# A streaming x + gamma * y: two DMA rings and a release through TensorE, against one ring in one fixed order

## The chip, the cores and the metric

The kernel runs on one core of a Trainium2 chip. The metric is device microseconds of one execution. The kernel before takes 119.98 us (median of 3 runs, 119.96 to 120.91). A profile adds its own number, the span from the first to the last instruction, which is about 1.3 us shorter than the time.

## The reference

```python
B, S, D = 1024, 16, 512          # x, y: bf16 [1024, 16, 512]; gamma: bf16 [512]
def reference(x, y, gamma):
    return x + gamma * y
```

That is 16.78 MB of x, 16.78 MB of y and 16.78 MB of output. There is one multiplication and one addition per element, so it is a streaming job.

## The kernel before

The 16384 rows of 512 elements are spread over 128 partitions, 128 rows in each. All of y (128 rows, 128 KB per partition) stays in on-chip memory and is overwritten with the result. For x there are only 75 rows of buffer. So x 64-117 goes into slots that x 0-53 has left, once the first addition has read them, and x 117-128 goes into 11 slots of its own. VectorE works in pieces of 53, 11, 53 and 11 rows.

Two engines issue transfers, SP (SyncE) and ACT (ScalarE). Each puts them into a queue of its own to the DMA engines, here called its ring; in the profile SP's is q1 and ACT's q10. The *release* is a signal that TensorE gives when x 64-117 has landed, and for which ACT waits before the first store and VectorE before it adds those rows.

```python
PIECES = [53, 11, 53, 11]
SP  = [('y', 0, 4), ('y', 4, 64), ('x', 0, 64, 0), ('y', 64, 128), ('x', 64, 117, 0), ('x', 117, 128, 64)]
ACT = [('g',), ('s', 0, 64), ('s', 64, 128)]      # gamma, then the two stores
EARLY = (2, 0)                                    # SP's first two issues go before the start barrier
RELEASE = ('x', 64, 117, 0)
DVE = [('m', 0), ('m', 1), ('a', 0), ('a', 1), ('m', 2), ('m', 3), ('a', 2), ('a', 3)]
# ... cut: buffers, semaphores, gamma broadcast through a matmul ...
    # in the ring of ACT, before the first store:
            if kind == "s" and not went:
                _take(s_go, 1, eng)
# ...
    # TensorE: when x 64-117 has landed, let ACT store and VectorE add
    _take(s_load[RELEASE], 16, nc.tensor)
    nc.tensor.sem_inc(s_go, 1)
    nc.tensor.sem_inc(s_rel, 1)
```

`('x', 64, 117, 0)` is a load of rows 64 to 117 of x into slot 0. `('s', 0, 64)` is the store of rows 0 to 64. `m` and `a` are the multiplication and addition of a piece. Each transfer is 128 contiguous runs, one per partition, and so eight per DMA engine. The trace records each such run as one packet.

## Time and profile before

| what | before |
|---|---|
| time, median of 3 | 119.98 us |
| span in the profile | 118.7 us |
| DMA queues, share of 16 engines | 66.0% + 32.6% |
| DMA rate over the span | 424 GB/s |
| VectorE busy | 70.0 us (59%) |
| x 117-128 issued, issue to landing | 56.1 us, 23.8 us |
| first store issued | 76.95 us (on ACT) |

The share of a DMA queue is the time that its packets were under way. The rate is the bytes divided by the span. The lines themselves stand in the prediction.

### The profile page before, as it was taken

The numbers are of one execution on the slowest core, as the hardware profiler recorded it, in microseconds if no ns is written. First come the engines' busy times: TensorE is split into PE (matmuls) and PEld (weight loads), VectorE is DVE, ScalarE is ACT, GpSimd is POOL, SyncE is SP. The second block draws the span as 40 slices with busy tenths as digits, with TensorE's granted clock in tenths as the row PEclk, the third lists the DMA queues.
The fourth block names the chain that finished last, engine by engine and source line by source line (L and its number), as shares of the span: only waits on it lengthen the run. The fifth ranks groups of instructions, "written<-read, shape, count | busy, mean of one in ns | idle before, by whom it ended". The sixth has DMA issues, their size and how long they took to land. (4 is left out here: it accounts for less than half of the span.)

```text
span 118.7 us, 80 instructions
## 1 busy us (share of the span) xinstructions
PE 0.6 (0%) x1; PEld 0.1 (0%) x1; DVE 70.0 (59%) x10; POOL 0.2 (0%) x4
## 2 busy tenths in 40 slices
PE   0001000000000000000000000000000000000000
PEld 0000000000000000000000000000000000000000
DVE  0002000599999299999759999999999910000000
POOL 0000000000000000000000000000000000000000
DMA  8977977998899888998896969498899889988891
GB/s 268 571 332 331 663 331 331 596 464 353 353 486 574 353 353 353 640 420 353 353 585 293 585 293 585 205 634 353 353 596 464 353 353 420 640 353 353 353 663 44
DMA packets 1154, 50.33 MB, mean 424 GB/s; under 512 B 129, under 2 KB 130, under 8 KB 258
## 3 DMA queue, kind: packets, MB, share of 16 engines
q1 hardware_dynamic: 864, 33.55, 66.0%
q10 hardware_dynamic: 290, 16.78, 32.6%
HBM read 33.56 MB, written 16.78 MB: 424 GB/s over the span
## 5 line engine op out<-in xcount | busy, mean ns | idle before, releaser
L156 DVE TENSOR_TENSOR y_sb<-y_sb,gamma_sb 128x27136 bf16<-128x27136 bf16 (+1 forms) x4 | 34.6, 8688 | 12.3 <-DVEq L25 12.3
L165 DVE TENSOR_TENSOR y_sb<-x_sb,y_sb 128x27136 bf16<-128x27136 bf16 (+1 forms) x4 | 34.6, 8689 | 2.3 <-DVEq L25 2.2
L132 DVE CAST gamma_sb<-gamma_ps 128x512 bf16<-128x512 f32 x1 | 0.7, 692 | 8.8 <-DVEq L25 8.8
L127 DVE MEMSET ones_row<- 1x128 bf16 x1 | 0.2, 165 | 2.0 <-PEq L41 2.0
L130 PE MATMUL gamma_ps<-gamma_row,ones_row 1*128 1x512 bf16 x1 | 0.6, 577 | 10.2 <-PEq L25 10.2
L130 PEld LDWEIGHTS gamma_ps<-gamma_row,ones_row 1*128 1x128 bf16 x1 | 0.1, 99 | 10.2 <-issue 10.2
L194 POOL MEMSET const-bfloat16-1.0<- 128x1 bf16 x1 | 0.1, 101 | 0.0
L194 POOL MEMSET const-uint8-127<- 128x1 uint8 x1 | 0.1, 101 | 0.0
L194 POOL MEMSET const-float32-0.0<- 128x1 f32 x1 | 0.1, 98 | 0.2 <-issue 0.2
L194 POOL MEMSET const-float32-1.0<- 128x1 f32 x1 | 0.1, 98 | 0.0
## 6 DMA issues: line engine op xcount, KB each, us to landing
y_sb<-in_y_dram SPq DMA_DIRECT2D x1, 7680.0 KB, 21.4
x_sb<-in_x_dram SPq DMA_DIRECT2D x1, 6784.0 KB, 20.8
x_sb<-in_x_dram SPq DMA_DIRECT2D x1, 1408.0 KB, 23.8
y_sb<-in_y_dram SPq DMA_DIRECT2D x1, 512.0 KB, 3.8
out_dram<-y_sb ACTq DMA_DIRECT2D x2, 22.8
x_sb<-in_x_dram SPq DMA_DIRECT2D x1, 39.3
gamma_row<-in_gamma_dram ACTq DMA_DIRECT2D x1, 1.0 KB
y_sb<-in_y_dram SPq DMA_DIRECT2D x1, 58.3
```

Source lines behind the costliest of these rows:

```text
L127: nc.vector.memset(ones_row, 1.0).then_inc(s_ones, 1)
L130: nc.tensor.matmul(gamma_ps, ones_row, gamma_row, start=True, stop=True).then_inc(s_ps, 1)
L132: nc.vector.tensor_copy(out=gamma_sb, in_=gamma_ps).then_inc(s_dve, 1)
L156: nc.vector.tensor_tensor(out=yt, in0=yt, in1=g, op=MULT).then_inc(s_dve, 1)
L165: nc.vector.tensor_tensor(out=yt, in0=xt, in1=yt, op=ADD).then_inc(s_add, 1)
L194: nc = _bacc.Bacc("TRN2", target_bir_lowering=False, num_devices=1)
```

## The change

The intent is simplicity: one ring, one order, no release. If a ring is served in order, stores placed behind the loads can't disturb them, and the detour through TensorE is not needed. The first y load also becomes one transfer.

```diff
-SP = [('y', 0, 4), ('y', 4, 64), ('x', 0, 64, 0), ('y', 64, 128), ('x', 64, 117, 0), ('x', 117, 128, 64)]
-ACT = [('g',), ('s', 0, 64), ('s', 64, 128)]
-EARLY = (2, 0)
-RELEASE = ('x', 64, 117, 0)
+RING = [("y", 0, 64), ("x", 0, 64, 0), ("y", 64, 128), ("x", 64, 117, 0),
+        ("x", 117, 128, 64), ("s", 0, 64), ("s", 64, 128)]      # all on SP
+EARLY = 1
 ...
-    _take(s_load[RELEASE], 16, nc.tensor)
-    nc.tensor.sem_inc(s_go, 1)
-    nc.tensor.sem_inc(s_rel, 1)
 ...
-                if w == RELEASE:
-                    _take(s_rel, 1, nc.vector)
-                else:
-                    _take(s_load[w], 16, nc.vector)
+                _take(s_load[w], 16, nc.vector)
```

Gamma's load stays on ACT. SP waits for the first addition before x 64-117, for the second before the first store, and for the fourth before the second store.

More of the change, by code (lines that the diff above doesn't have):

```diff
@@ L6 @@
 PIECES = [53, 11, 53, 11]
-SP = [('y', 0, 4), ('y', 4, 64), ('x', 0, 64, 0), ('y', 64, 128), ('x', 64, 117, 0), ('x', 117, 128, 64)]
-ACT = [('g',), ('s', 0, 64), ('s', 64, 128)]
-EARLY = (2, 0)
-RELEASE = ('x', 64, 117, 0)
-DVE = [('m', 0), ('m', 1), ('a', 0), ('a', 1), ('m', 2), ('m', 3), ('a', 2), ('a', 3)]
+RING = [
+    ("y", 0, 64),
+    ("x", 0, 64, 0),
+    ("y", 64, 128),
+    ("x", 64, 117, 0),
+    ("x", 117, 128, 64),
+    ("s", 0, 64),
+    ("s", 64, 128),
+]
+EARLY = 1
+DVE = [("m", 0), ("m", 1), ("a", 0), ("a", 1), ("m", 2), ("m", 3), ("a", 2), ("a", 3)]
 MULT, ADD = mybir.AluOpType.mult, mybir.AluOpType.add
@@ L59 @@
     y_sb = nc.alloc_sbuf_tensor("y_sb", [P, rows, D], dt).ap()
-    x_loads = [w for w in SP + ACT if w[0] == "x"]
-    y_loads = [w for w in SP + ACT if w[0] == "y"]
-    stores = [w for w in SP + ACT if w[0] == "s"]
-    for loads in (x_loads, y_loads, stores):
-        assert sum(w[2] - w[1] for w in loads) == rows
+    x_loads = [w for w in RING if w[0] == "x"]
+    y_loads = [w for w in RING if w[0] == "y"]
+    stores = [w for w in RING if w[0] == "s"]
+    for transfers in (x_loads, y_loads, stores):
+        assert sum(w[2] - w[1] for w in transfers) == rows
     x_rows = max(w[3] + w[2] - w[1] for w in x_loads)
@@ L71 @@
     s_load = {w: sem("s_" + "_".join(map(str, w[:2]))) for w in x_loads + y_loads}
-    s_add, s_go, s_rel, s_end, s_out = sem("s_add"), sem("s_go"), sem("s_rel"), sem("s_end"), sem("s_out")
-    added = [a for kind, *a in DVE if kind == "a"]
-    order = {a[0]: k for k, a in enumerate(added)}
+    s_add, s_out = sem("s_add"), sem("s_out")
+    added = [c for kind, c in DVE if kind == "a"]
+    order = {c: k for k, c in enumerate(added)}
     def meets(a, b, c, d):
@@ L94 @@
     early = []
-    def ring(eng, what, n_early):
-        known, went = 0, False
-        for k, w in enumerate(what):
-            kind = w[0]
-            need = frees(w) if kind == "x" else pieces_of(w[1], w[2]) + list(w[3:]) if kind == "s" else []
-            need = max((order[c] + 1 for c in need), default=0)
-            if kind == "s" and not went:
-                _take(s_go, 1, eng)
-                went = True
-            if need > known:
-                eng.wait_ge(s_add, need)
-                known = need
-            if kind == "g":
-                i = eng.dma_start(out=gamma_row, in_=gamma.unsqueeze(0)).then_inc(s_gamma, 16)
-            elif kind == "x":
-                to = x_sb[:, w[3] : w[3] + w[2] - w[1], :]
-                i = eng.dma_start(out=to, in_=xv[:, w[1] : w[2], :]).then_inc(s_load[w], 16)
-            elif kind == "y":
-                r = slice(w[1], w[2])
-                i = eng.dma_start(out=y_sb[:, r, :], in_=yv[:, r, :]).then_inc(s_load[w], 16)
-            else:
-                r = slice(w[1], w[2])
-                i = eng.dma_start(out=ov[:, r, :], in_=y_sb[:, r, :]).then_inc(s_out, 16)
-            if k < n_early:
-                early.append(i.ins)
-    ring(nc.sync, SP, EARLY[0])
-    ring(nc.scalar, ACT, EARLY[1])
+    known = 0
+    for k, w in enumerate(RING):
+        kind, r = w[0], slice(w[1], w[2])
+        need = frees(w) if kind == "x" else pieces_of(w[1], w[2]) if kind == "s" else []
+        need = max((order[c] + 1 for c in need), default=0)
+        if need > known:
+            nc.sync.wait_ge(s_add, need)
+            known = need
+        if kind == "x":
+            to = x_sb[:, w[3] : w[3] + w[2] - w[1], :]
+            i = nc.sync.dma_start(out=to, in_=xv[:, r, :]).then_inc(s_load[w], 16)
+        elif kind == "y":
+            i = nc.sync.dma_start(out=y_sb[:, r, :], in_=yv[:, r, :]).then_inc(s_load[w], 16)
+        else:
+            i = nc.sync.dma_start(out=ov[:, r, :], in_=y_sb[:, r, :]).then_inc(s_out, 16)
+        if k < EARLY:
+            early.append(i.ins)
+    nc.scalar.dma_start(out=gamma_row, in_=gamma.unsqueeze(0)).then_inc(s_gamma, 16)
     nc.vector.memset(ones_row, 1.0).then_inc(s_ones, 1)
@@ L133 @@
     _take(s_dve, 1, nc.vector)
-    _take(s_load[RELEASE], 16, nc.tensor)
-    nc.tensor.sem_inc(s_go, 1)
-    nc.tensor.sem_inc(s_rel, 1)
     landed, open_mults = set(), 0
-    def need(loads, c):
-        for w in loads:
+    for kind, c in DVE:
+        for w in y_loads if kind == "m" else x_loads:
             if w not in landed and meets(starts[c], starts[c + 1], w[1], w[2]):
-                if w == RELEASE:
-                    _take(s_rel, 1, nc.vector)
-                else:
-                    _take(s_load[w], 16, nc.vector)
+                _take(s_load[w], 16, nc.vector)
                 landed.add(w)
-    for kind, *args in DVE:
-        c = args[0]
         yt = y_sb[:, starts[c] : starts[c + 1], :]
         if kind == "m":
-            need(y_loads, c)
             g = gamma_sb[:, None, :].to_broadcast([P, PIECES[c], D])
@@ L158 @@
         else:
-            need(x_loads, c)
             if open_mults:
@@ L165 @@
             nc.vector.tensor_tensor(out=yt, in0=xt, in1=yt, op=ADD).then_inc(s_add, 1)
-    nc.scalar.sem_inc(s_end, 1)
-    _take(s_end, 1, nc.sync)
     _take(s_add, n, nc.sync)
```

## The prediction

> **What bounds the kernel now.** The median is 119.98 us and the profiled span 118.7 us, so 1.3 us lies outside what the profile shows. I read the page first: busy time, slices, DMA queues.
>
> ```profile
> PE 0.6 (0%) x1; PEld 0.1 (0%) x1; DVE 70.0 (59%) x10; POOL 0.2 (0%) x4
> DVE  0002000599999299999759999999999910000000
> DMA  8977977998899888998896969498899889988891
> q1 hardware_dynamic: 864, 33.55, 66.0%
> q10 hardware_dynamic: 290, 16.78, 32.6%
> HBM read 33.56 MB, written 16.78 MB: 424 GB/s over the span
> ```
>
> No compute engine is near full: VectorE works 59% of the span and has nothing to do in the last seven slices. The two DMA queues (q1 is SP's ring with all loads, q10 is ACT's with gamma and the stores) add up to 66.0 + 32.6 = 98.6% of 16 engines' time. The bytes are fixed by the task: 16.78 MB each of x, y and output. So the kernel is bound by the DMA engines, and only their gaps can be won.
>
> The chain of waits is of no help: its last piece is the last addition, and the 23 us of store after it are not in it. So I went to the timeline, for the slack of each transfer's issue.
>
> ```profile
> 0.00 0.84 SPq L116 DMA_DIRECT2D y_sb<-in_y_dram  x2
> 1.90 0.33 SPq L113 DMA_DIRECT2D x_sb<-in_x_dram  x1
> 2.28 0.51 SPq L116 DMA_DIRECT2D y_sb<-in_y_dram  x1
> ...
> 21.99 17.29 DVE L156 TENSOR_TENSOR y_sb<-y_sb,gamma_sb 128x27136 bf16<-128x27136 bf16 x2 [10.33 <-DVEq L25]
> 41.46 17.29 DVE L165 TENSOR_TENSOR y_sb<-x_sb,y_sb 128x27136 bf16<-128x27136 bf16 x2 [2.17 <-DVEq L25]
> 55.78 0.81 SPq L113 DMA_DIRECT2D x_sb<-in_x_dram  x2
> 60.69 17.29 DVE L156 TENSOR_TENSOR y_sb<-y_sb,gamma_sb 128x27136 bf16<-128x27136 bf16 x2 [1.94 <-DVEq L25]
> 76.95 18.85 ACTq L119 DMA_DIRECT2D out_dram<-y_sb  x2
> 78.13 17.30 DVE L165 TENSOR_TENSOR y_sb<-x_sb,y_sb 128x27136 bf16<-128x27136 bf16 x2
> ```
>
> The reader is to compare each issue with the time at which the engines run dry. The trace's DMA packet records give the second time. One engine's 65536-byte packets start 2.415 us apart, the 61440-byte ones 2.264, the 54272-byte ones 2.004, the 11264-byte ones 0.419, the 4096-byte ones 0.155. Each transfer is 128 packets, eight per engine:
>
> - y 0-4: 8 x 0.155 = 1.24; y 4-64: 8 x 2.264 = 18.11
> - x 0-64 and y 64-128: 8 x 2.415 = 19.32 each
> - x 64-117: 16.03; x 117-128: 3.35
> - two stores: 19.32 each
>
> The sum is 116.0 us. The first packet starts 1.00 us into the span, the slowest engine's last at 118.33, so 117.3 us of engine time hold 116.0 us of steady work. The rest is start-up (the first 4096-byte packets took up to 1.16 us instead of 0.16) and the engines' stagger. The last landing counts 118.67. Between transfers an engine loses about 6 ns: a completion packet of 9 ns, then the next transfer's first packet.
>
> The slack: x 64-117 is issued at 55.78, and y 64-128's last data leave the engines at about 60.0, so there are 4.2 us to spare; the second store is issued at about 95.5, after the last addition (78.13 + 17.30 = 95.43), and the first store's data end at 98.4 to 99.0, so about 2.9. Against this, the lead that a new transfer needs is about 1.0 us, from the first issue to the first packet.
>
> **What the Trainium skill says.** "DMA: Bandwidth & Descriptors", section "Where 436 GB/s comes from", gives 435 GB/s for the 16 engines together. The trace agrees: 16 x 65536 B / 2.415 us = 434 GB/s in the steady state, so the rate has nothing left in it.
>
> The same page, section "Issuing engines are not separate DMA queues", says that transfers issued by SP, ACT and GpSimd run on the same 16 engines, and that issuing from several only saves sequencer time. Here an issue takes 0.33 to 0.52 us on a sequencer that is otherwise waiting, so a second ring saves nothing that is short.
>
> The same page, section "Queues, rings and completion order", says that an engine consumes one ring in order and takes turns between rings packet by packet. The trace agrees with the first: load follows load in the order of issue. The second shows only weakly: the first store went out at 76.95 with x 117-128 unfinished, but no store packet started before an engine had done all of that load (first one at 79.06).
>
> **The change part by part.**
>
> 1. *First y load in one transfer.* Eight packets of 65536 B (19.32 us) replace 1.24 + 18.11 = 19.35 us and one completion packet (15 ns with its gap). Gain 0.03 to 0.05 us. The start-up latency is paid once either way. SP's first issue stays first, so the first packet should again start near 1.0 us. SP issues one transfer fewer before the common barrier (0.42 us less); x 0-64 goes out at about 1.5 instead of 1.90, but behind 19 us of queued data: worth nothing.
>
> 2. *First multiply.* It waits for rows 0-64 of y as before (the 53-row piece spans both old transfers), so it starts at about 22.0. Gamma is ready at 10.97 + 0.69 = 11.66; even if its 1 KB waits one or two more 2.4 us packets, there are some 5 us left.
>
> 3. *Release through TensorE gone.* Before, TensorE waited for x 64-117 (landed 76.60), then let ACT issue the first store and VectorE go on. VectorE was in its multiplies until 60.69 + 17.29 = 77.98 and started the addition at 78.13, so the detour cost it nothing. Gain 0.0.
>
> 4. *First store on SP's ring.* It needs the first two additions (41.46 + 17.29 = 58.75), so SP issues it at about 58.8 instead of 76.95, right behind x 117-128. As the ring is served in order, its first packet still starts when the engines finish that load, near 79.06. Gain 0.0, since the engines already changed over with no gap.
>
> 5. *Second store on SP's ring.* It waits for the same last addition, ready at about 95.4, and lies behind a store with 2.9 us left. Gain 0.0.
>
> 6. *Tail.* One semaphore step between ACT and SP goes; it was passed some 23 us before the end. Gain 0.0.
>
> Sum: 119.98 - 0.05 = 119.93 us. The instructions on VectorE, their shapes and order are unchanged; the built programs show that SP keeps seven rows, ACT loses its two stores, and nothing else moves.
>
> **The rivals.**
>
> *The stores are not kept behind the loads.* If the first store, now free 18 us earlier, shared the engines with x 64-117, that load would take about twice its 16 us, landing near 93 instead of 76.6. The last two additions would end 17.3 us later, at 110, while all but the last store is done at 99; the engines would stand idle for 11 us and the time would be about 131 us. This is what the release of before guarded against with its two rings. Against it: one ring, in which the trace of before shows strict order for six transfers.
>
> *The change from load to store costs something inside one ring*[...]. If every engine waited once for a fresh issue, as at the start, it would lose about 1 us: 121.0. Against it: seven or eight packets per engine are queued per transfer, and load follows load on one ring with 6 ns lost. No trace here shows a store behind a load on the same ring, so this one I can't exclude.
>
> *SP is held at an issue because its ring is full*, and the second store goes out late. At about 58.8 an engine would hold 8 + 8 + 8 packets of the two x loads and the first store, plus the rest of y. Before, four transfers (32 packets per engine) were put on the same ring within 2.8 us without an issue stretching beyond 0.51 us. And 2.9 us of slack lie before any of it shows.
>
> *The start changes.* Big packets may fill the pipeline better or worse than 4096-byte ones: the engines' first y transfer took 0.5 to 1.0 us longer than its steady time. If half of that were won or lost: 119.4 to 120.5.
>
> *The opposite hope*, that removing waits and a detour speeds up the end, fails on the sum: 116.0 us of data at a rate that is already the ceiling, and all waits removed are hidden.
>
> **Range and chances.** The centre is 119.93. Downward, only part of the 1.3 us that are not steady data can go, so 119.5 is the low end. Upward, one of three runs before was 120.91, 0.9 us above the others, and the load-to-store rival adds up to 1 us; as a median of three hides a single bad run, I take 120.6. To be faster by 2% (below 117.6) the kernel would have to beat its own steady data time plus start and tail, so 0.01. Slower by 2% (above 122.4) needs the first rival or several small ones: 0.02. The rest, 0.97, is within 2%.
>
> **What would show it.** In the changed kernel's profile: DMA still about 424 GB/s over the span and the two queues together still about 98.6%, now some 99% of it on SP's; VectorE's groups with the same durations and starts near 22.0, 41.4, 60.6 and 78.1; stores on SP's queue at about 58.8 and 95.5, the first with some 40 us to landing instead of 23. The steps are wrong if x 64-117 lands clearly after 76.6 (stores mixing with loads), if slices near 79 us fall below the others (a gap at the change-over), if the second store goes out clearly after the last addition (ring full), or if the first y load lands more than 0.5 us away from 22.0 (the start).

## More of the kernel before

One more view is needed later, the list of DMA issues: what moves, the issuing queue, the size, and the microseconds from issue to landing. For the two late x loads it reads, in the kernel before:

```profile
x_sb<-in_x_dram SPq DMA_DIRECT2D x1, 6784.0 KB, 20.8
x_sb<-in_x_dram SPq DMA_DIRECT2D x1, 1408.0 KB, 23.8
```

The first is x 64-117, the second x 117-128. They are issued together and served one after the other.

## The result and the profile after

| | before | changed |
|---|---|---|
| time, median of 6 | 119.97 us (119.83 to 120.91) | 120.81 us (120.66 to 120.92) |
| ratio | | 1.0069, interval 1.0045 to 1.0093 |
| span in the profile | 118.7 us | 119.5 us |

The change costs 0.8 us. It is within 2%, but above the predicted range (119.5 to 120.6).

The page of the changed kernel, DMA lines:

```profile
DMA  9899888988899889988897979698899888998892
q1 hardware_dynamic: 1008, 50.33, 98.6%
q10 hardware_dynamic: 2, 0.00, 0.0%
HBM read 33.56 MB, written 16.78 MB: 421 GB/s over the span
```

All traffic is now on q1, SP's ring, as meant. The share is 98.6%, as it was in sum before, and no slice has a hole. Yet the rate is 421 GB/s instead of 424. The engines are as busy as before and move less, so some packets took longer. A gap would have shown in the share; this loss does not.

The timeline of the changed kernel:

```profile
0.00 0.38 SPq L110 DMA_DIRECT2D y_sb<-in_y_dram  x1
...
22.00 17.29 DVE L135 TENSOR_TENSOR y_sb<-y_sb,gamma_sb 128x27136 bf16<-128x27136 bf16 x2 [11.09 <-DVEq L28]
41.43 17.29 DVE L143 TENSOR_TENSOR y_sb<-x_sb,y_sb 128x27136 bf16<-128x27136 bf16 x2 [2.14 <-DVEq L28]
55.74 0.81 SPq L108 DMA_DIRECT2D x_sb<-in_x_dram  x2
58.75 37.02 SPq L112 DMA_DIRECT2D out_dram<-y_sb  x2
60.66 17.29 DVE L135 TENSOR_TENSOR y_sb<-y_sb,gamma_sb 128x27136 bf16<-128x27136 bf16 x2 [1.94 <-DVEq L28]
78.10 17.30 DVE L143 TENSOR_TENSOR y_sb<-x_sb,y_sb 128x27136 bf16<-128x27136 bf16 x2
```

VectorE's groups begin within 0.03 us of where they began before (21.99, 41.46, 60.69 and 78.13). The second store is issued right after the last addition. Only the first store moved, from 76.95 to 58.75. So neither VectorE nor SP lost the 0.8 us. The list of DMA issues has it:

```profile
x_sb<-in_x_dram SPq DMA_DIRECT2D x1, 6784.0 KB, 20.8
x_sb<-in_x_dram SPq DMA_DIRECT2D x1, 1408.0 KB, 24.7
```

x 64-117 landed as before; x 117-128 took 0.9 us longer, from the same issue time. This is the last load in front of the first store. The packet records (11264 B each, eight per engine) show how. One engine's eight, in ns (the records name no engine; these follow one another without a gap):

```
before     422 422 422 422 422 422 422 422
changed    422 422 422 775 879 655 552 422
```

Taken over all engines, the excess over 422 ns sums to 0.81 us per engine, against 0.01 us before. On each engine the slow packets begin at 76.7 to 77.8 us, some 2 us before the load's data would have ended (79.1 to 79.6). After them everything runs at full speed, 0.8 us late to the end: the first store's data now end at 99.2 to 99.8 us instead of 98.4 to 99.0. This "excess", always of the last load in front of the store, is the measure in all experiments below. Each kernel has one trace, so each excess is a single reading.

### The profile page after: what moved, and what is told of

Same layout as the page of the kernel before. It is cut to its first block, busy times and chain, and to the rows that moved or that the text cites. A ratio compares the mean times of both kernels' runs of the same rounds, so it can differ in the third digit from the quotient of the medians.

```text
span 119.5 us, 72 instructions
## 1 busy us (share of the span) xinstructions
PE 0.6 (0%) x1; PEld 0.1 (0%) x1; DVE 70.0 (59%) x10; POOL 0.2 (0%) x4
## 3 DMA queue, kind: packets, MB, share of 16 engines
q1 hardware_dynamic: 1008, 50.33, 98.6%
```

## The experiments

Two theories after reading the traces. A: the loss comes from the first store lying behind the load, and is a matter of where (same ring) or when (too early) it is queued. B: it comes from the y load or the start. Sixteen kernels ran, all with correct results.

### The y load alone, and the ring alone

`y_one` is the kernel before with only the first y load merged:

```diff
-SP = [('y', 0, 4), ('y', 4, 64), ('x', 0, 64, 0), ...
-EARLY = (2, 0)
+SP = [('y', 0, 64), ('x', 0, 64, 0), ...
+EARLY = (1, 0)
```

> Kernel before with one change: y 0-64 as one transfer of 65536-byte packets. Theory A (the loss of 0.8 us comes from the first store lying behind the 11-row x load on the same ring): no loss, 119.9 to 120.0, and the 11-row load again takes about 3.4 us from its first packet to its completion packet. Rival B (the loss comes from the start, or from the row count of the first load): 120.7 to 120.9.

Measured: 120.02 us, before 119.89, ratio 0.9995 (0.9959 to 1.0032); excess 0.00.

`ring_y_split` is the changed kernel with only the y load split again:

```diff
-    ("y", 0, 64),
+    ("y", 0, 4),
+    ("y", 4, 64),
-EARLY = 1
+EARLY = 2
```

> Changed kernel with the first y load split again into 4 and 60 rows, both issued early; stores stay on SP's ring, no release. Theory A: the loss stays, 120.7 to 120.9, and the packets of the 11-row load are again slow (0.5 to 0.9 us instead of 0.42). Rival B: back to 119.9 to 120.0.

Measured: 120.81 us, ratio 1.0063 (1.0026 to 1.0101); excess 1.07 us. The two together acquit the y load: merging it costs nothing that can be seen, and splitting it again brings nothing back. B falls.

### The ring, or the moment of the issue

`ring_gated` is the changed kernel, stores on SP's ring, with the old release put back in front of the first store:

```diff
+RELEASE = ("x", 64, 117, 0)
+FIRST_STORE = ("s", 0, 64)
+        if w == FIRST_STORE:
+            _take(s_go, 1, nc.sync)
+    _take(s_load[RELEASE], 16, nc.tensor)      # TensorE, as before
+    nc.tensor.sem_inc(s_go, 1)
+    nc.tensor.sem_inc(s_rel, 1)
```

> Changed kernel, stores on SP's ring, but the first store is issued only when x 64-117 has landed (about 76.9 us instead of 58.75), passed through TensorE as in the kernel before. If the loss comes from the store being queued already when the 11-row load begins (theory A1, timing): 119.9 to 120.2, with at most one slow packet per engine. If it comes from sharing one ring whenever the store is issued (A2): 120.7 to 120.9.

Measured: 120.04 us, ratio 1.0001 (0.9963 to 1.0038); excess 0.00, not one slow packet. The store is issued at 76.98. In its timeline and then in its list of issues:

```profile
76.98 18.86 SPq L117 DMA_DIRECT2D out_dram<-y_sb  x2
```

```profile
x_sb<-in_x_dram SPq DMA_DIRECT2D x1, 1408.0 KB, 23.8
```

The 11-row load is back at 23.8 us, though the store follows it on the same ring. So the ring is not the cause; the moment is. `small_first` asks whether the small packets of the 11-row load matter:

```diff
-    ("x", 64, 117, 0),
     ("x", 117, 128, 64),
+    ("x", 64, 117, 0),
-DVE = [..., ("m", 3), ("a", 2), ("a", 3)]
+DVE = [..., ("m", 3), ("a", 3), ("a", 2)]
```

> Changed kernel with the two last x loads swapped: the 11-row load goes before the 53-row load, which is then the one ahead of the store; VectorE adds piece 3 before piece 2, so that its end stays near 95.4. If the loss needs small packets ahead of the store (A-small): 119.9 to 120.1, no slow packets. If any load ahead of a store queued on the same ring loses the same time (A-any): 120.7 to 120.9, and the last packets of 54272 bytes are slow by about 0.8 us in sum. If only the row count or the place in memory of the 11-row load matters: its packets are slow in the new place too, 120.7.

Measured: 120.79 us, ratio 1.0058 (1.0017 to 1.0098). The 11-row load is now clean (0.02 us) and the 53-row load has the excess, 0.95 us per engine. Nearly all of it is in each engine's last packet: 2.59 to 3.23 us instead of 2.004. The loss goes to whatever load is last in front of the store, large or small.

### How early is too early

`small_first_gated` releases the store when the 11-row load lands, with the 53-row load already under way:

```diff
 (small_first with the release of ring_gated)
+RELEASE = ("x", 117, 128, 64)
```

> Kernel small_first (53-row x load last) with the first store issued only when the 11-row load has landed, about 64.2, when the 53-row load is already running and 15 us from its end. Theory R: the loss stays, 120.6 to 120.9, one slow packet of about 2.9 us at the end of each engine's share. Rival (a store has to be queued before the load in front of it begins): 119.9 to 120.1.

Measured: 120.86 us, ratio 1.0065 (1.0051 to 1.0078); the store is issued at 64.27, excess 0.76 us, again in the last packets. `gate_46` brings the release closer to the end of the loads:

```diff
 (ring_gated)
-    ("x", 64, 117, 0),
+    ("x", 64, 110, 0),
+    ("x", 110, 117, 46),
-RELEASE = ("x", 64, 117, 0)
+RELEASE = ("x", 64, 110, 0)
```

> One ring, first store released through TensorE as in ring_gated, but 2.1 us earlier: the 53-row x load is split into 46 and 7 rows and the landing of the 46 releases the store, issued at about 74.8, some 4.2 us before the loads' data end. Theory R (the store is harmful when the engines find it at the moment their reading passes the end of the loads, about 2 us before the loads' records end): the loss of 0.8 us is back, 120.7 to 120.9, with slow packets from about 77. Rival (it's harmful only when queued long ahead, or before the 11-row load itself is queued up to start): 119.9 to 120.1.

Measured: 120.77 us, ratio 1.0062 (1.0050 to 1.0075); excess 0.64 us. Its timeline has the store only 2.2 us earlier than in ring_gated, and that is enough:

```profile
74.78 20.98 SPq L118 DMA_DIRECT2D out_dram<-y_sb  x2
```

`late_gate` goes the other way and releases the store only when the last load has landed:

```diff
 (ring_gated)
-RELEASE = ("x", 64, 117, 0)
+RELEASE = ("x", 117, 128, 64)
```

> One ring, first store issued only when the 11-row load, the last one, has landed (about 79.9). Measures the lead that a store needs: with the 1.0 us between issue and first packet seen at the start, the engines stand idle from 79.0-79.6 to about 80.9, 1.3 to 1.9 us, so 121.2 to 121.9 in all. If stores need less lead than loads: 120.5 to 121.0. No slow packets in the 11-row load in either case.

Measured: 121.81 us, ratio 1.0146 (1.0132 to 1.0161); excess 0.02 us. Here the loss is a gap: the loads' data end at 79.10 to 79.58, the store is issued at 80.26 and its first packet starts at 81.10:

```profile
80.26 15.47 SPq L117 DMA_DIRECT2D out_dram<-y_sb  x2
```

That gives the lead of a store on idle engines, 0.84 us, and the price of an idle turn, 1.8 us.

`act_ungated` puts the stores back on ACT's ring but leaves the release out, the prediction's first rival:

```diff
 (changed kernel; the stores leave SP's ring)
+    for w in stores:
+        nc.scalar.wait_ge(s_add, max(order[c] + 1 for c in pieces_of(w[1], w[2])))
+        nc.scalar.dma_start(out=ov[:, r, :], in_=y_sb[:, r, :]).then_inc(s_out, 16)
```

> Changed kernel with its stores on ACT's ring again, but without the release: the first store is issued at about 58.75. Prediction's first rival (two rings share the engines): packets of store and x 64-117 alternate, the x load lands near 93 instead of 76.6, 128 to 132. Rival (a store queued early costs the same 0.8 us wherever it is queued, and the loads still go first): 120.7 to 120.9.

Measured: 133.94 us, ratio 1.1154 (1.1127 to 1.1181), with one slow run of 142.71 left out of the ratio. From its page (busy tenths in 40 slices, and the issue of x 64-117), then its timeline:

```profile
DMA  9997997978979979779796979697890004979777
x_sb<-in_x_dram SPq DMA_DIRECT2D x1, 6784.0 KB, 38.3
```

```profile
55.76 0.81 SPq L109 DMA_DIRECT2D x_sb<-in_x_dram  x2
58.77 53.24 ACTq L122 DMA_DIRECT2D out_dram<-y_sb  x2
60.68 17.30 DVE L142 TENSOR_TENSOR y_sb<-y_sb,gamma_sb 128x27136 bf16<-128x27136 bf16 x2 [1.95 <-DVEq L28]
94.34 17.29 DVE L150 TENSOR_TENSOR y_sb<-x_sb,y_sb 128x27136 bf16<-128x27136 bf16 x2 [16.37 <-DVEq L28]
```

VectorE waits 16.37 us for x 64-117, and later the engines are idle for three slices and part of a fourth, until the last addition frees the second store. In the packet records of an engine, packets of 54272 B (load) and 65536 B (store) alternate one by one from about 64 us on. So the release was needed with two rings, and one ring does replace it for the order. It has a second effect that shows here too: once, just before the first store packets, the load's packets are slow (excess 0.60 us per engine); in the 30 us of alternation after that they are not.

### What about the queued store does it

Four kernels queue a transfer of two rows (256 KB, eight packets of 2048 B per engine) behind the 11-row load at 56.6 us, on top of ring_gated. They differ in what it moves: a piece of the store, a load, a copy within the on-chip memory, a copy within DRAM.

In short:

```diff
 (early_store2)                       (the three others)
-    ("s", 0, 64),                   +    ("c", 0, 2),          # before the first store
+    ("s", 0, 2),                    +    early_load2:      out=scratch,            in_=xv[:, 0:2, :]
+    ("s", 2, 64),                   +    early_sbuf_copy:  out=scratch,            in_=y_sb[:, 0:2, :]
+FIRST_STORE = ("s", 2, 64)          +    early_hbm_copy:   out=ov[:, 126:128, :],  in_=xv[:, 0:2, :]
```

The last copy writes wrong values into two rows of the output; the second store waits for it and writes them again.

> Kernel ring_gated, but two rows of the first store (256 KB, eight packets of 2048 B per engine) are issued early, at about 56.6, right behind the 11-row load; the other 62 rows stay behind the release. If any store behind the loads, however small, costs the whole 0.8 us: 120.7 to 120.9, slow packets in the 11-row load. If the loss grows with the store data that the engines can fetch ahead: near 120.1 to 120.4, fewer slow packets.

> Control: ring_gated with a two-row load (256 KB, DRAM to SBUF, of x into a scratch) queued at the same place instead. It adds 8 packets of 2048 B per engine, some 0.65 us at the rate of the 4096-byte packets, so 120.6 to 120.8, and no slow packets in the 11-row load.

> The same with a two-row copy from SBUF to SBUF. If fetching from SBUF behind loads is what slows the loads' end: slow packets in the 11-row load as in early_store2, and a time above the control by as much. If it is the writing to DRAM: no slow packets, the time of the control.

> The same with a two-row copy from DRAM (x) to DRAM (rows of the output that the second store writes later, after waiting for this copy). If writing to DRAM is what slows the loads' end: slow packets in the 11-row load, and a time above the control; if it is fetching from SBUF: none.

Measured: 120.42 us (excess 0.40), 121.43 (0.37), 121.17 (0.51), 121.15 (0.55). The control failed: the plain load has excess as well, and its time is the longest of the four although its excess is the smallest. So these four alone decide nothing. The reason I give for the excess is that the two rows move the end of the loads back by 0.67 us, so that the released store (issued at 77.09) comes that much earlier relative to that end. In the next four, the release comes after the landing of the 11-row load, as in late_gate, so that only the small transfer lies behind the loads:

```diff
 (early_store2, early_load2, early_sbuf_copy, early_hbm_copy)
-RELEASE = ("x", 64, 117, 0)
+RELEASE = ("x", 117, 128, 64)
```

> Kernel late_gate (no slow packets: 0.02 us of excess in the 11-row load per engine) with two rows of the store issued early behind the loads. If store behind load is the cause: slow packets in the 11-row load, 0.3 to 0.8 us of excess per engine. Time near late_gate's 121.8 plus the excess.

> Control: late_gate with a two-row load behind the loads. If the excess of early_load2 (0.37 us) came from the released store: no excess now, below 0.05 us. If any small transfer at the end of the queue makes it: 0.3 to 0.4 again. Time near 121.8 + 0.67 = 122.5 plus the excess.

> late_gate with a two-row copy from SBUF to SBUF behind the loads. If fetching from SBUF is the cause: excess as in late_store2. If writing to DRAM is: below 0.05 us, and 122.5.

> late_gate with a two-row copy from DRAM to DRAM behind the loads. If writing to DRAM is the cause: excess as in late_store2. If fetching from SBUF is: below 0.05 us, and 122.5.

Measured, two runs each, with the one trace of each:

| kernel | from, to | time | excess in the 11-row load | slow packets (over 490 ns) of 128 |
|---|---|---|---|---|
| late_load2 | DRAM, SBUF | 121.87 us | 0.00 us | 0 |
| late_hbm_copy | DRAM, DRAM | 121.89 us | 0.04 us | 3 |
| late_sbuf_copy | SBUF, SBUF | 122.15 us | 0.24 us | 21 |
| late_store2 | SBUF, DRAM | 121.57 us | 0.31 us | 20 |

(late_store2 is quicker in total than late_gate, 121.81, because two rows of its store go out in the idle turn. The extra 256 KB of late_load2 fit into that turn too and cost nothing, so the 122.5 expected were missed.) The lists of issues agree for the 11-row load; late_load2, late_hbm_copy, late_sbuf_copy and late_store2:

```profile
x_sb<-in_x_dram SPq DMA_DIRECT2D x1, 1408.0 KB, 23.8
scratch<-in_x_dram SPq DMA_DIRECT2D x1, 256.0 KB, 24.0
```

```profile
x_sb<-in_x_dram SPq DMA_DIRECT2D x1, 1408.0 KB, 23.8
out_dram<-in_x_dram SPq DMA_DIRECT2D x1, 256.0 KB, 24.0
```

```profile
x_sb<-in_x_dram SPq DMA_DIRECT2D x1, 1408.0 KB, 24.1
scratch<-y_sb SPq DMA_DIRECT2D x1, 256.0 KB, 24.2
```

```profile
x_sb<-in_x_dram SPq DMA_DIRECT2D x1, 1408.0 KB, 24.2
out_dram<-y_sb SPq DMA_DIRECT2D x1, 256.0 KB, 24.4
```

In these four traces the two transfers that fetch from on-chip memory (SBUF) slow the load ahead of them; the two that fetch from DRAM do not, whether they write to DRAM or not. So it is the fetching side that matters here. The times of the three with extra bytes agree: the copy from SBUF is the slowest in both of its runs. With 256 KB it costs 0.2 to 0.3 us, with a whole store 0.8.

## Why the prediction was wrong

**Right.** The bound (the DMA engines), the unchanged course of VectorE, the worthlessness of the y merge and of the earlier second issue, and the second store's slack were as told: y_one, ring_y_split and the timeline show them. The first rival was right too, as a road not taken: 133.9 us measured against an estimate of 131, with the x load landing 17.5 us late (94.1, from 55.76 and 38.3 us to landing, instead of 76.6).

**The step that failed** is part 4: "As the ring is served in order, its first packet still starts when the engines finish that load, near 79.06. Gain 0.0". The order was kept, but the load itself finished 0.8 us later, so the first store packets came at 79.9. Serving in order does not mean that a queued store leaves the load ahead of it alone. Part 3 failed with it: "the detour cost it nothing" was true of VectorE, but the release also held the store back until 2 us before the loads' end, and that was worth 0.8 us. I had counted what the wait delayed and not what it protected. None of the four signs that the prediction named as its undoing appeared (x 64-117 landed at 76.6, no slice near 79 us fell, the second store went out on time, the first multiply began at 22.00). Only the rate, 421 instead of 424 GB/s, and x 117-128, which it did not watch, gave the step away.

The second rival had the size nearly right (1 us, measured 0.8), but by luck, since its reason was wrong. It expected a fresh start at the change-over within one ring. There was no gap there (9 ns of completion packet, then the store), ring_gated changes over on one ring at no cost, and act_ungated pays 0.6 us with two rings. The range then left this rival out at the top, although the text says that it could not be excluded; 121.0 belonged inside.

**What is shown in its place.** The table orders the kernels by the moment at which the engines can have the first store. This is an estimate: issue plus the 0.84 us measured in late_gate. It is set against the middle of the loads' undisturbed end, 79.3 us from late_gate (80.0 where two more rows are loaded or copied):

| kernel | store issued | engines have it before the loads' end | excess |
|---|---|---|---|
| changed | 58.75 | 19.7 us | 0.81 us |
| small_first_gated | 64.27 | 14.2 us | 0.76 us |
| gate_46 | 74.78 | 3.7 us | 0.64 us |
| early_hbm_copy (end moved to 80.0) | 76.94 | 2.2 us | 0.55 us |
| early_load2 (end moved to 80.0) | 77.09 | 2.0 us | 0.37 us |
| ring_gated | 76.98 | 1.5 us | 0.00 us |
| before (on ACT) | 76.95 | 1.5 us | 0.01 us |
| late_gate | 80.26 | after it | 0.02 us, but a gap |

ring_y_split (1.07 us) and small_first (0.95) issue the store as early as the changed kernel. early_sbuf_copy and early_store2 are left out, since they fetch from on-chip memory early in any case.

In these traces the step lies between 1.5 us (nothing) and 2.0 us (0.37), near where the slow packets of the changed kernel begin. In act_ungated, too, they start at 61.7 to 62.2, 2.1 to 2.6 us after the engines could have its store (58.77 + 0.84 = 59.6), although packets of 2 us are a coarse ruler. A reading that fits, but is not shown: an engine fetches some 2 us ahead of what its records show; when its fetching runs past the last load and finds a store, it goes on with fetches from on-chip memory while the last load data are still on their way, and these are then slowed. A store that arrives later finds those data already fetched and still starts without a gap, because it needs only 0.84 us. The Trainium skill supports the ingredients: "DMA: Bandwidth & Descriptors", section "Two DMAs through the same engine are not ordered", says that the read and write sides of an engine are separate queues and descriptors are pipelined; section "Latency and other measured facts" gives an HBM access latency of 2 us at high load, against 0.2 us on average. No run here measures the reading side or that latency by itself.

**Not shown.** Why fetches from on-chip memory slow loads that are already on their way stays open; so does why the loss happens once and not again in the alternation of act_ungated. The four late_ kernels have one trace and two timed runs each. The kernel before itself had one run of 120.91 among 6 and one of 121.41 among 11, for which there is no trace. No version beat the kernel before: ring_gated and y_one tie with it (1.0001 and 0.9995).

## What to carry to other kernels

When a wait or a release is removed because nothing waits for it any longer, ask also what it kept from starting. In a kernel that streams in and then out at the DMA limit, try several moments for the first store. Here an issue 2.3 us before the end of the last load's data cost nothing. An issue 4.5 us or more before it cost 0.7 to 0.9 us even on one ordered ring, one after the last load had landed cost 1.8 us of idle engines, and on two rings far too early cost 14 us. Closer to that end than 2.3 us nothing was tried, and no run shows that these distances hold for other sizes. A loss of this kind does not lower the DMA engines' busy share; look at bytes per second and at issue-to-landing of single transfers.

## What the Trainium skill lacked or had wrong

- "DMA: Bandwidth & Descriptors", sections "Queues, rings and completion order" and "Two DMAs through the same engine are not ordered", treat order and completion, but not that a transfer fetching from SBUF, queued behind loads from DRAM, slows their last 2 us: 0.64 to 1.07 us for a whole store on one ring (five traces), 0.24 to 0.31 us for 256 KB, nothing for transfers that fetch from DRAM (0.00 and 0.04 us).
- The same page, section "Issuing engines are not separate DMA queues", says that issuing from several engines only saves the sequencer's time. With the store issued at 77 us the two agree (120.02 us on two rings in y_one, 120.04 on one in ring_gated). It says too that such transfers interleave, but not what that can cost when one of them is waited for: the same transfers, with the store queued at 58.75 us, took 120.81 us on one ring and 133.94 us on two.
- The same page, section "Queues, rings and completion order", gives about 9 to 17 descriptors as a typical packet between two turns of an engine. With runs of 54272 and 65536 B the two rings alternated one run at a time in the records of act_ungated. If a record is one descriptor, which the trace does not say, that is 1 and not 9 to 17.
